# Two weight matrices loaded by a casting DMA from GpSimd instead of a plain DMA, staging tiles and cast operations

## The chip, the cores and the metric

The kernel runs on one core of one Trainium2 chip. The metric is device time in microseconds (us). TensorE is called PE, VectorE DVE, ScalarE ACT, GpSimd POOL and SyncE SP, as in the profile. A run is "fast" or "slow" by its state: a slow run took more than 1.5% longer than the fastest run of the same kernel.

## The reference, cut to what matters

```python
# attention: B=4, heads H=8, S=768, D=48; one state [D, D] for each head
for t in range(S):
    cur = einsum('bhd,bhe->bhde', u * k_t, v_t)
    y[:, :, t] = einsum('bhd,bhde->bhe', r_t, state + cur)
    state = w_t[..., None] * state + einsum('bhd,bhe->bhde', k_t, v_t)
# MLP on x = y as [3072 tokens, 384]
h = x @ w_in            # 384 x 2048
g = maximum(h, 0) ** 2
out = g @ w_out         # 2048 x 384
```

All inputs and the output are fp32 in HBM. The two weight matrices are 3.1 MB each.

## The kernel before

The 768 positions of the four sequences are cut into 24 steps of 128 tokens. A step loads four tiles (w, r, k, v) of 192 KB. Each is 1024 rows of 192 bytes, because one token of one head is 48 floats. The weights come in eight DMAs of 768 KB, with rows of 2 KB (w_in) or 1.5 KB (w_out), through the same sync queue. They land in fp32 staging tiles, and 28 copies on ACT and DVE turn them into bf16.

```python
def load_one(dst, src, b, c):                      # L69: the loads of a step
    nc.sync.dma_start(
        out=dst, in_=src[b, :, c * C:(c + 1) * C, :].rearrange("h c d -> c h d"))
...
def load_wi(g):                                    # L95; load_wo is alike
    w_st["i", g] = stage_pool.tile([C, KT, GW], FP32, name="w_st")
    nc.sync.dma_start(
        out=w_st["i", g][:],
        in_=moe_w_in[:, g * GW:(g + 1) * GW].rearrange("(a p) f -> p a f", p=128))
...
def cast(eng, kind, g, j):                         # L108
    dst = wi_sb[:, :, g * GW:(g + 1) * GW] if kind == "i" else wo_sb[:, g * 4:(g + 1) * 4, :]
    copy = nc.scalar.copy if eng == "A" else nc.vector.tensor_copy
    copy(dst[:, j], w_st[kind, g][:, j])
```

The order of instructions is not written by hand. The kernel holds a small list scheduler: each operation has an engine, an assumed duration, a rank, dependencies, and PSUM buffers that it takes or gives. While the program is built, the scheduler plays the operations through in assumed time, and each engine gets its instructions in the order found. On the chip every engine then runs its list in that order, whatever happens to the loads. Three parts matter below:

```python
# PSUM pool "cp" has ONE buffer. cum_ takes it and rd_ gives it back; p_ takes it, pm_ gives it back
op("P", .44, at, cum_, (s,), [("lw_", s)], take="cp")                  # needs w of step s
op("V", .95, at - 90, rd_, (s,), [("exp_", s), ("ld", s, "k")] + ..., give="cp")   # needs k of step s
op("P", .33, at + 5, p_, (s,), [("rkt_", s)], take="cp")
...
seq = [(0, x) for x in "wrkvu"] + [(1, x) for x in "wrkv"] + [(g, "i") for g in range(4)]
seq += [(2, x) for x in "wrkv"] + [(g, "o") for g in range(4)]
seq += [(s, x) for s in range(3, NSTEP) for x in "wrkv"]
last = []
for n, x in seq:                                   # assumed: one load after the other
    free = ...
    op("S", {"i": 2.08, "o": 2.08, "u": .65}.get(x, 1.25), 0, ld, (n, x), last + free)
    last = [("ld", n, x)]
```

The chain of one step runs: loads, cum_ (PE), exp_ (ACT), rd_ (DVE), tr_ (PE, transposes), rkt_ (DVE), p_ (PE), pm_ (DVE), y_ (PE), ysb_ (DVE), yt_ (PE), xt_ (ACT). After xt_ of a block's steps, m1_ (first MLP product) and m2_ (second) can run. The first MLP block is steps 0 and 1. In gaps before the first m2_ the scheduler inserts warm-up matmuls, whose results are not used.

## Time and profile before

The kernel before took 219.09 us (median of 2 runs, 218.32 to 219.87).

| before | value | view |
|---|---|---|
| span | 214.2 us | page |
| PE, DVE, ACT, POOL busy | 197.1, 152.7, 127.5, 84.1 us | page, busy times |
| PE busy in 0 to 40 us; of it warm-up matmuls | 35.02; 17.92 us | windows |
| first m1_ | 21.65 us | timeline of PE |
| all casts on ACT / DVE | 7.8 / 5.3 us | groups of instructions |

The first fence is the head of the page: busy time of each engine with its share of the span, then tenths of busy time (and of granted PE clock) in 40 slices.

```profile
span 214.2 us, 5655 instructions
PE 197.1 (92%) x2232; PEld 140.4 (66%) x2232; DVE 152.7 (71%) x279; ACT 127.5 (60%) x255; POOL 84.1 (39%) x105
...
PE   7898997987899997989999999999999999999983
...
PEclk9999999999999999999999999999999999999999
```

PE is the engine that sets the end: from 120 us to 205 us it is busy without a gap. So the time is decided by what PE loses earlier. The next fence is the table of windows: length, then busy time and number of instructions for each engine, granted clock, DMA share, GB/s written.

```profile
0.00:10.00 10.00, 7.78 (x50) 3.39 (x51) 3.52 (x8) 3.71 (x6) 4.59 (x15) 1.00 0.91 164
10.00:20.00 10.00, 10.00 (x97) 5.35 (x94) 7.61 (x15) 3.52 (x7) 4.89 (x7) 1.00 1.01 327
20.00:30.00 10.00, 8.98 (x89) 6.71 (x88) 7.24 (x15) 8.43 (x18) 2.89 (x3) 1.00 0.97 269
30.00:40.00 10.00, 8.27 (x99) 5.86 (x98) 6.20 (x16) 7.46 (x17) 2.28 (x3) 1.00 0.84 221
```

A busy PE is not a working PE here. Of the 35.02 us in this stretch, 17.92 are warm-up matmuls, so the useful part is 17.1 us, and 22.9 of the 40 us are lost. The DMA share shows why: the loads keep the DMA engines busy at 0.84 to 1.01. Below, idle time plus warm-up time is called *lost PE time*. Over the whole span of before it is 214.2 - 197.1 + 17.9 = 35.0 us.

The timeline of SP shows how the one queue orders the loads (start, duration, instruction; a long duration is an issue that stalls):

```profile
5.52 2.33 SPq L69 DMA_DIRECT2D rk_raw<-in_k_dram  x1
...
8.64 3.06 SPq L95 DMA_DIRECT2D w_st<-in_moe_w_in_dram  x4
11.75 0.51 SPq L69 DMA_DIRECT2D w_raw<-in_w_dram  x1
12.30 5.18 SPq L69 DMA_DIRECT2D rk_raw<-in_r_dram  x1
17.53 4.29 SPq L69 DMA_DIRECT2D rk_raw<-in_k_dram  x1
```

The loads of step 1 go ahead of the weights, and the loads of step 2 stall behind the weights for 5.2 and 4.3 us. A weight DMA takes about 1.95 us at the 400 GB/s that the windows show from 16 to 18 us (its landings lie 2.0 to 3.1 us apart, with ramps at both ends), and a step load 1.0 us, when each has the DMA engines to itself. The timeline of PE has p_ of step 1 at 16.32 and the first MLP product at 21.65:

```profile
16.32 0.40 PE L210 MATMUL cp<-rkT 64*128 64x128 bf16 x8
...
21.65 1.47 PE L288 MATMUL m<-xT,wi_sb 128*128 128x256 bf16 x12 [1.02 <-ACT xT L273]
```

### The profile page before, as it was taken

To read this page: it belongs to the slowest core of one execution; us is meant where nothing else is said; L and a number is where in the kernel's file an instruction comes from. 1 tells how busy PE (TensorE), PEld (TensorE's weight loads), DVE (VectorE), ACT (ScalarE), POOL (GpSimd) and SP (SyncE) were. 2 spreads that over 40 slices of the span, in tenths; PEclk is the share of its full clock that TensorE was granted. 3 is DMA by queue.
4 is the path that set the end of the run, shared out by engine and by line. 5 is a ranking of instruction groups with operands and counts; after the bars stand their busy time and mean duration, and the time that the engine had idled before them with its cause. 6 is when DMAs were issued, how large, how long until landed. Compare 5 with 4: busy or idle time off the path is not lost.

```text
span 214.2 us, 5655 instructions
## 1 busy us (share of the span) xinstructions
PE 197.1 (92%) x2232; PEld 140.4 (66%) x2232; DVE 152.7 (71%) x279; ACT 127.5 (60%) x255; POOL 84.1 (39%) x105
## 2 busy tenths in 40 slices
PE   7898997987899997989999999999999999999983
PEld 2454765555677675766766677777777777777751
DVE  3475795646898989879859989989886775533310
ACT  3353966644856767477685576667847546555540
POOL 5371320546556639655565655557112010000000
PEclk9999999999999999999999999999999999999999
DMA  7999899779987999699889997983101100111112
GB/s 135 195 307 344 207 383 219 153 164 193 177 152 150 181 163 171 135 200 160 172 167 195 142 203 147 193 176 76 40 2 41 37 11 28 40 37 37 40 37 73
DMA packets 107177, 30.43 MB, mean 142 GB/s; under 512 B 100368, under 2 KB 105616, under 8 KB 107152
## 3 DMA queue, kind: packets, MB, share of 16 engines
q1 hardware_dynamic: 107152, 30.09, 67.1%
q8 instruction: 17, 0.28, 0.6%
q14 instruction: 8, 0.07, 0.1%
HBM read 25.36 MB, written 4.72 MB: 140 GB/s over the span
## 4 chain that ended last, share of the span: by engine, by line
PE 46%; SPq 13%; DMA 13%; DVE 10%; issue 7%; POOL 6%; ACT 3%; DVEq 0%; POOLq 0%
PE m L307 19%; PE m L288 17%; SPq L69 10%; DMA w_st<-in_moe_w_out_dram 4%; DVE gt L300 4%; DMA w_raw<-in_w_dram 3%; DMA v_raw<-in_v_dram 3%; POOL qprod L161 2%; DVE pmT L216 2%; PE tr L198 2%; POOL ku L157 2%; DMA rk_raw<-in_r_dram 2%; POOL vq L169 2%; PE cp L210 1%; SPq L95 1%
## 5 line engine op out<-in xcount | busy, mean ns | idle before, releaser
L288 PE MATMUL m<-xT,wi_sb 128*128 128x256 bf16 (+1 forms) x672 | 76.5, 257 | 4.2 <-ACT xT L273 2.9
L295 ACT ACTIVATE rl<-m 128x512 f16<-128x512 f32 x96 | 56.5, 597 | 37.5 <-PE m L288 36.4
L307 PE MATMUL m<-wo_sb,gt 128*128 128x384 bf16 x384 | 74.9, 326 | 1.2 <-ACT o_sb L312 0.6
L288 PEld LDWEIGHTS <-wi_sb 128*128 128x128 bf16 x672 | 57.7, 98 | 17.1 <-issue 5.4
L300 DVE TENSOR_TENSOR gt<-rl 128x512 bf16<-128x512 f16 x96 | 54.7, 584 | 19.8 <-ACT rl L295 19.2
L307 PEld LDWEIGHTS <-gt 128*128 128x128 bf16 x384 | 35.3, 98 | 19.7 <-DVE gt L300 1.3
L157 POOL TENSOR_TENSOR ku<-rk_raw,u_bc 128x384 f32<-128x384 f32 x24 | 24.8, 1034 | 42.1 <-DMA rk_raw<-in_k_dram 37.3
L216 DVE TENSOR_TENSOR pmT<-cp,tri_strict 128x512 bf16<-128x512 f32 x48 | 30.8, 681 | 3.6 <-PE cp L210 3.6
L189 DVE TENSOR_TENSOR rdec_buf<-rk_raw,cp 128x768 bf16<-128x768 f32 x24 | 22.8, 948 | 11.2 <-ACT cp L185 9.0
L169 POOL TENSOR_TENSOR vq<-v_raw,q 128x384 f32<-128x384 f32 x24 | 21.6, 901 | 18.8 <-DVE y_sb L261 8.6
L161 POOL TENSOR_TENSOR qprod<-rk_raw,ku 128x384 f32<-128x384 f32 x24 | 25.1, 1048 | 1.2
L238 POOL TENSOR_TENSOR S<-t_state,a_c 128x192 bf16<-128x192 f32 x20 | 11.0, 548 | 29.3 <-DVE t_state L234 16.7
L185 ACT ACTIVATE cp<-cp 128x768 f32<-128x768 f32 x24 | 19.1, 795 | 0.8
L321 PE MATMUL m<-warm 128*128 128x512 bf16 x64 | 17.9, 416 | 1.2 <-DVE warm L129 1.2
L202 DVE COPY rkT<-tr 128x1024 bf16<-128x1024 bf16 x24 | 16.4, 682 | 3.7 <-PE tr L198 3.7
L149 ACT ACTIVATE lw_buf<-w_raw 128x384 bf16<-128x384 f32 x24 | 12.5, 521 | 8.4 <-DMA w_raw<-in_w_dram 8.2
L153 ACT CAST v_bf<-v_raw 128x384 bf16<-128x384 f32 x24 | 12.2, 508 | 8.4 <-DMA v_raw<-in_v_dram 7.7
L312 ACT ACTIVATE o_sb<-m 128x384 f32<-128x384 f32 x24 | 11.8, 491 | 8.2 <-PE m L307 7.6
L165 DVE TENSOR_REDUCE q<-qprod 128x8 f32<-128x384 f32 x24 | 13.1, 545 | 4.4 <-POOL qprod L161 4.1
L198 PE MATMUL tr<-ident,rdec_buf 128*128 128x128 bf16 x192 | 14.8, 220 | 1.3 <-DVE rdec_buf L189 1.0
L261 DVE TENSOR_TENSOR y_sb<-vq,y 128x384 bf16<-128x384 f32 x24 | 13.1, 547 | 2.2 <-PE y L255 2.1
L198 PEld LDWEIGHTS <-rdec_buf 128*128 128x128 bf16 x192 | 11.5, 98 | 4.1 <-DVE rdec_buf L189 2.0
(40 smaller groups left out, 142.9 us busy)
## 6 DMA issues: line engine op xcount, KB each, us to landing
w_raw<-in_w_dram SPq DMA_DIRECT2D x24, 192.0 KB, 4.3
rk_raw<-in_r_dram SPq DMA_DIRECT2D x24, 192.0 KB, 4.2
rk_raw<-in_k_dram SPq DMA_DIRECT2D x24, 192.0 KB, 4.3
v_raw<-in_v_dram SPq DMA_DIRECT2D x24, 192.0 KB, 4.1
out_dram<-o_sb SPq DMA_DIRECT2D x24, 192.0 KB, 2.0
w_st<-in_moe_w_in_dram SPq DMA_DIRECT2D x4, 768.0 KB, 8.5
w_st<-in_moe_w_out_dram SPq DMA_DIRECT2D x4, 768.0 KB, 8.6
u_bc<-in_u_dram SPq DMA_DIRECT2D x1, 192.0 KB, 4.6
```

Of the source, the lines that this page charges most:

```text
L69: nc.sync.dma_start(out=dst, in_=src[b, :, c * C:(c + 1) * C, :].rearrange("h c d -> c h d"))
L157: nc.gpsimd.tensor_mul(ku[:], raw["rk", s][:, 1], u_bc[:])
L161: nc.gpsimd.tensor_mul(qp[:], raw["rk", s][:, 0], tiles.pop(("ku", s))[:])
L169: nc.gpsimd.tensor_mul(vq[:], raw["v", s][:], tiles.pop(("q", s))[:, :, None].to_broadcast([C, H, D]))
L185: nc.scalar.activation(cs[:, :, 0:DM], cs[:, :, 0:DM], AF.Exp)
L189: nc.vector.tensor_mul(rdec[:, :, :, 0:D], raw["rk", s][:], tiles.pop(("cs", s))[:, :, 0:DM].rearrange("p a (h d) -> p a h d", h=H))
L198: nc.tensor.transpose(ps_tr[:, i, p, :], rdec[:, i, 2 * p:2 * p + 2, :], ident[:])
L216: nc.vector.tensor_mul(tiles["pmT", s][:, e], tiles["p", s][:, e].rearrange("p (a t) -> p a t", a=HP), tri_strict[:, None, :].to_broadcast ...
L288: nc.tensor.matmul(ps1[:, j, :], wi_sb[:, kk, n * 128:(n + 1) * 128], xT[:, kk, s0 * C:s0 * C + width], start=(kk == 0), stop=(kk == KT - 1))
L295: nc.scalar.activation(rl[:], tiles.pop(("m1", i, g))[:], AF.Relu, scale=RS)
L300: nc.vector.tensor_mul(tiles["gt", i][:, g * ng:(g + 1) * ng, :], rl[:], rl[:])
L307: nc.tensor.matmul(tiles["m2"][:], gt[:, n, mt * 128:(mt + 1) * 128], wo_sb[:, n, :], start=(n == 0), stop=(n == NT - 1))
```

## The change

The intent is to take the 28 casts off ACT and DVE, to free eight staging buffers of 6 KB per partition, and to take the weights out of the sync queue. The weights are cast during the DMA. That forces GpSimd as the issuing engine: the Trainium skill, "DMA: Bandwidth & Descriptors", section "SWDGE vs HWDGE vs iDMA", lists a cast during DMA as "SWDGE only (GpSimd)". Line numbers after the change are lower by 1 to 9.

```diff
-    stage_pool = ctx.enter_context(tc.tile_pool(name="stage", bufs=8))
...
     def load_wi(g):
-        w_st["i", g] = stage_pool.tile([C, KT, GW], FP32, name="w_st")
-        nc.sync.dma_start(
-            out=w_st["i", g][:],
+        nc.gpsimd.dma_start(
+            out=wi_sb[:, :, g * GW:(g + 1) * GW],
             in_=moe_w_in[:, g * GW:(g + 1) * GW].rearrange("(a p) f -> p a f", p=128))
...                                                   (load_wo alike; cast() and its 28 operations removed)
-            deps += [("cast", "AV"[ch % 2], "i", ch, j) for j in range(KT)]
+            deps.append(("ld", ch, "i"))
...
-    last = []
+    last, lastg = [], [("ku_", 0)]
     for n, x in seq:
         free = ...
-        op("S", {"i": 2.08, "o": 2.08, "u": .65}.get(x, 1.25), 0, ld, (n, x), last + free)
+        if x in "io":
+            op("G", 1.0, -100, ld, (n, x), lastg)
+            lastg = [("ld", n, x)]
+            continue
+        op("S", {"u": .65}.get(x, 1.25), 0, ld, (n, x), last + free)
...                                                   (in make_order)
-                           done[d] + (hop if plan[d][0] != e else 0) > now + 1e-6 for d in deps):
+                           done[d] + (hop if plan[d][0] != e else 0) > now + 1e-6
+                           for d in deps if not (e == "G" and fn is ld)):
...
-                    end = done[key] = free_at[e] = now + us
+                    end = free_at[e] = now + us
+                    if fn is ld and e == "G":
+                        landed[0] = max(landed[0], end + 1) + 4.2
+                        end = landed[0]
+                    done[key] = end
```

The last hunks are part of the change and turn out to carry about half of the loss (e3 below). The scheduler waives the dependencies of the GpSimd loads, so all eight stand ahead of the first GpSimd product. It assumes that a weight lands every 4.2 us, and that step loads beside them still take 1.25 us each.

## The prediction

> **What bounds the kernel now.** TensorE (PE). The page's busy table gives PE 92% of a 214.2 us span, DVE 71%, ACT 60%, GpSimd (POOL) 39%. By windows, it is full from 120 us to the end, so the end is set by what PE loses earlier. In 0 to 40 us PE is busy 35.0 us, but 17.9 us of that are warm-up matmuls (L321): about 23 us lost. The first MLP matmul (L288) starts at 21.65, the first of L307 at 30.8. What holds the start is loading: the DMA share is 0.84 to 1.01 in every 10 us of the first 40. A backlogged load of 192 KB moves at about 195 GB/s (1.0 us), a weight load of 768 KB at 390 to 410 GB/s (1.95 us). All DMAs go through one queue in order; the loads of step 2 wait on the sync queue for 5.2 and 4.3 us behind weights.
>
> **Removed.** 28 casts: ACT 6 x 0.61 + 8 x 0.51 = 7.8 us, DVE 6 x 0.42 + 8 x 0.35 = 5.3 us, all between 14 and 37 us, where neither engine is the limit. Worth 1 to 2 us at most: a shorter gap from landing to use.
>
> **Added.** Eight weight DMAs issued from GpSimd. In the instruction order of the changed kernel they stand, without a wait, ahead of the first ku product, so they start at about 3.5 us. I estimate 1 to 2 us of GpSimd each; the first ku, at 8.2 us today, starts at 12 to 18.
>
> **Moved.** HBM is still read for 6.3 MB of fp32 weights; only the SBUF write halves. The Trainium skill, "DMA: Bandwidth & Descriptors", "Queues, rings and completion order", says that each DMA engine alternates between queues packet by packet. A weight row is 1.5 or 2 KB, a step row 192 B, so I expect the weights to take half to four fifths of the engines until they are in, at 24 to 36 us. No trace here shows it.
>
> **The critical step.** The new order assumes step loads unaffected: it puts PE work of steps 2, 3 and 4 ahead of or between the first MLP matmuls, and PE is in order. The transposes of step 3 stand before the second MLP group. Their input cannot land before 16 loads x 1.0 + 8 x 1.95 + 1.9 = 33.5 us unless weights lag; fair shares give about 31. That makes the early MLP groups 8 to 12 us later than that order intends. Earlier weights and step loads not queued behind them win most of it back (my estimate: 7 us), so I expect a net loss of 0 to 5 us. If the two queues overlap, the loss turns into a gain of up to 7 us.
>
> **Predicted:** 220 us, 8 in 10 within 210 to 231. Faster by over 2%: 0.28; within 2%: 0.37; slower by over 2%: 0.35.
>
> **What would show it.** Right: r, k and v of steps 0 to 2 take over 6 us to land while weights are in flight; the first L288-type matmul starts after 28 us; PE idles more than 23 us in 0 to 40; the first GpSimd product after 12 us. Wrong: step loads land in 4 to 5 us beside weights and the DMA total exceeds 300 GB/s until 25 us, with MLP starting by 25 us: then about 211.
>
> **What would make it wrong.** Overlap of the two queues (faster); a cast that slows the DMA itself, or slow descriptor generation on GpSimd, delaying w_out or the first products (slower, 230); later slack that absorbs the late start.

## The result, and the profile after

The changed kernel took 226.98 us (2 runs, 226.86 and 227.10), with correct results. The ratio of fast runs is 1.047, 95% interval 1.0389 to 1.055: slower. A ratio here is the mean time of one kernel's fast runs over that of the other's of the same rounds, so it is not quite the ratio of the medians quoted.

For this pair the difference is large. The two runs of before that are listed give 226.98 / 219.09 = 1.036. The 1.047 must rest on further runs of before. The profiled one, with a span of 214.2 us, is one of these: spans lie about 2 us below times (225.1 below 227.10), so it took some 216 us (an estimate). In the four later jobs before took 215.2 to 217.1 us, which puts 226.98 at 4.5 to 5.5% over it. "Slower" holds either way; its size is good to about a point.

| | before | after |
|---|---|---|
| span | 214.2 | 225.1 us |
| useful PE time in 0 to 40 us | 35.02 - 17.92 = 17.1 | 24.45 - 18.29 = 6.2 us |
| PE idle in 40 to 150 us | 110 - 101.81 = 8.2 | 110 - 103.11 = 6.9 us |
| lost PE time, whole span | 35.0 | 225.1 - 198.3 + 18.8 = 45.6 us |
| first m1_ | 21.65 | 40.39 us |
| ACT + DVE busy | 280.2 | 264.5 us |

The casts are indeed gone: ACT and DVE together are 15.7 us less busy, of which the casts were 7.8 + 5.3 = 13.1. The span grew by 10.9 us all the same, and lost PE time grew by 10.6 us, all of it in the first 40 us. Head of the page and DMA queues of after:

```profile
span 225.1 us, 5614 instructions
PE 198.3 (88%) x2222; PEld 140.8 (63%) x2225; DVE 144.0 (64%) x265; ACT 120.5 (54%) x241; POOL 89.4 (40%) x113
...
PE   7708069999798799997999999799999999999983
...
PEclk9976658999999999999999999999999999999999
...
q1 hardware_dynamic: 103440, 23.80, 56.0%
q0 software_dynamic: 3712, 3.15, 8.7%
```

The same windows after:

```profile
0.00:10.00 10.00, 7.72 (x51) 3.48 (x53) 3.98 (x8) 3.29 (x5) 9.43 (x22) 1.00 0.92 161
10.00:20.00 10.00, 4.68 (x25) 2.04 (x25) 1.00 (x3) 1.49 (x3) 2.10 (x3) 0.72 1.23 187
20.00:30.00 10.00, 3.23 (x14) 1.33 (x12) 2.54 (x4) 0.43 (x1) 2.77 (x3) 0.67 1.18 182
30.00:40.00 10.00, 8.82 (x83) 4.63 (x86) 5.38 (x11) 3.99 (x10) 4.97 (x6) 0.75 1.02 176
```

Apart from warm-up matmuls, every compute engine is nearly empty from 10 to 30 us while the DMA share is above 1. The GB/s column counts bytes written, and a cast weight writes half of what it reads, so the fall from 327 to 187 GB/s does not mean that the reads slowed as much. The timeline of POOL shows the issues and the first products:

```profile
3.39 3.24 POOL L92 DMA_DIRECT2D wi_sb<-in_moe_w_in_dram  x4
6.62 3.00 POOL L97 DMA_DIRECT2D wo_sb<-in_moe_w_out_dram  x4
9.61 1.04 POOL L148 TENSOR_TENSOR ku<-rk_raw,u_bc 128x384 f32<-128x384 f32 x1
...
26.74 0.99 POOL L148 TENSOR_TENSOR ku<-rk_raw,u_bc 128x384 f32<-128x384 f32 x1 [14.13 <-DMA rk_raw<-in_k_dram]
```

The sync queue stalls on step loads while the weights are in flight:

```profile
5.69 5.90 SPq L68 DMA_DIRECT2D rk_raw<-in_k_dram  x1
11.63 4.07 SPq L68 DMA_DIRECT2D v_raw<-in_v_dram  x1
15.75 7.19 SPq L68 DMA_DIRECT2D w_raw<-in_w_dram  x1
22.98 4.35 SPq L68 DMA_DIRECT2D rk_raw<-in_r_dram  x1
```

**How the two queues shared the DMA engines.** Adding the time to landing to each issue, the eight weights landed at 10.6, 13.1, 15.7, 18.2, 20.8, 23.4, 26.3 and 28.9 us: 2.6 us apart, against about 1.95 alone (1.93 for casting DMAs in e1 below), so they had 75% of the engines. The step loads beside them landed at 9.4 (u), 15.8, 21.3, 26.7 (w, r, k of step 1): 6.4, 5.5 and 5.4 us apart, against 1.0 alone, or 19% from r on. The sum is 94%, so the two queues do not add up to more than one. The split is what alternation row by row gives. A DMA engine handles 24 rows of 2 KB of a w_in DMA in 1.95 us, 81 ns each, and 32 rows of a w_out DMA, 61 ns each. It handles 64 rows of a step load in 1.0 us, 16 ns each. My estimate for one for one is therefore 64 x (81 + 16) = 6.2 us for a step load beside w_in and 64 x (61 + 16) = 4.9 us beside w_out; measured is 6.4 for the load beside w_in and 5.4 beside w_out. The trace also shows the turns directly. The packets of the two queues from 10 to 26 us (queue, packets, MB, share of the engines' time) are:

```profile
q0 software_dynamic: 2911, 2.42, 93.3%
q1 hardware_dynamic: 2915, 0.55, 31.4%
```

That is one for one; but for a few packets of 4 bytes that end each DMA, a packet is a row. This agrees with the Trainium skill, "DMA: Bandwidth & Descriptors", section "Queues, rings and completion order": an engine takes turns between its queues, a packet at a time. A small row pays for a large one.

**From the late load to the late MLP.** k of step 1 lands at 26.7 instead of 11.0 us. In the table of waits of after from 8 to 40 us (engine and tile, what it waited for, total us, times, longest us), the two largest are:

```profile
DVE rdec_buf L180 <- DMA rk_raw<-in_k_dram: 16.1, 2, 15.8
POOL ku L148 <- DMA rk_raw<-in_k_dram: 14.1, 1, 14.1
```

That is a delay of 15.7 us at the start of step 1's chain, but the first MLP product is 18.7 us late. The timeline of PE after shows a second delay inside the chain:

```profile
27.80 1.03 PE L189 MATMUL tr<-ident,rdec_buf 128*128 128x128 bf16 x8 [6.03 <-DVE rdec_buf L180]
...
30.91 0.27 PE L167 MATMUL cp<-ones_col,lw_buf 128*128 128x1 bf16 x4 [1.64 <-ACT lw_buf L140]
...
35.48 0.40 PE L201 MATMUL cp<-rkT 64*128 64x128 bf16 x8
...
40.39 0.81 PE L279 MATMUL m<-xT,wi_sb 128*128 128x256 bf16 x6
```

L189 is tr_ of step 1, L167 the head of cum_ of step *2*, L201 p_ of step *1*. The timeline of DVE has the copy that p_ of step 1 needs, at 28.87, and what stands between:

```profile
28.87 0.69 DVE L193 COPY rkT<-tr 128x1024 bf16<-128x1024 bf16 x1 [0.67 <-PE tr L189]
...
33.39 0.95 DVE L180 TENSOR_TENSOR rdec_buf<-rk_raw,cp 128x768 bf16<-128x768 f32 x1 [0.35 <-DMA rk_raw<-in_k_dram]
```

p_ of step 1 had its input at 28.87 + 0.69 = 29.56, but ran at 35.48. The planned order puts cum_ of step 2 ahead of it. cum_ waits for w of step 2, which landed at 30.3. It then holds the single cp buffer until rd_ of step 2 has run, and rd_ waits for k of step 2, which landed at 33.3. rd_ ended at 34.34; the last 1.1 us before p_ are yt_ of step 0 and three warm-up matmuls, which the order also puts ahead of it. In the assumed times both loads were long in by then. This is how an order made for other landings costs time: not where the load is late, but where something that could run stands behind it.

### The profile page after: what moved, and what is told of

It reads as the page before. It is cut to its first block, busy times and chain, and to the rows that moved or that the text cites. A ratio compares the mean times of both kernels' runs of the same rounds, so it can differ in the third digit from the quotient of the medians.

```text
span 225.1 us, 5614 instructions
## 1 busy us (share of the span) xinstructions
PE 198.3 (88%) x2222; PEld 140.8 (63%) x2225; DVE 144.0 (64%) x265; ACT 120.5 (54%) x241; POOL 89.4 (40%) x113
## 3 DMA queue, kind: packets, MB, share of 16 engines
q0 software_dynamic: 3712, 3.15, 8.7%
## 4 chain that ended last, share of the span: by engine, by line
PE 58%; DMA 12%; SPq 7%; DVE 7%; issue 5%; POOL 5%; ACT 4%; DVEq 0%; POOLq 0%; ACTq 0%
PE m L279 21%; PE m L298 20%; DMA w_raw<-in_w_dram 10%; SPq L68 6%; PE tr L189 4%; PE m L312 2%; PE cp L201 2%; POOL qprod L152 2%; DVE gt L291 2%; DMA v_raw<-in_v_dram 2%; PE tr L216 2%; DVE rdec_buf L180 2%; DVE pmT L207 1%; PE tr L261 1%; PE y L238 1%
## 5 line engine op out<-in xcount | busy, mean ns | idle before, releaser
L279 PE MATMUL m<-xT,wi_sb 128*128 128x256 bf16 (+1 forms) x672 | 76.4, 257 | 0.3 <-ACT rl L286 0.3
L298 PE MATMUL m<-wo_sb,gt 128*128 128x384 bf16 x384 | 75.8, 326 | 0.7 <-ACT o_sb L303 0.6
L291 DVE TENSOR_TENSOR gt<-rl 128x512 bf16<-128x512 f16 x96 | 50.7, 538 | 27.6 <-ACT rl L286 27.5
L279 PEld LDWEIGHTS <-wi_sb 128*128 128x128 bf16 x672 | 57.9, 98 | 13.0 <-issue 0.7
L298 PEld LDWEIGHTS <-gt 128*128 128x128 bf16 x384 | 35.1, 98 | 17.8 <-issue 1.0
L160 POOL TENSOR_TENSOR vq<-v_raw,q 128x384 f32<-128x384 f32 x24 | 20.9, 870 | 26.0 <-DVE y_sb L252 14.8
L189 PE MATMUL tr<-ident,rdec_buf 128*128 128x128 bf16 x192 | 15.2, 224 | 9.0 <-DVE rdec_buf L180 8.4
L140 ACT ACTIVATE lw_buf<-w_raw 128x384 bf16<-128x384 f32 x24 | 12.6, 524 | 18.7 <-DMA w_raw<-in_w_dram 18.7
L312 PE MATMUL m<-warm 128*128 128x512 bf16 x54 | 18.8, 483 | 1.5 <-DVE warm L120 1.2
L189 PEld LDWEIGHTS <-rdec_buf 128*128 128x128 bf16 x192 | 11.6, 99 | 12.5 <-DVE rdec_buf L180 9.8
L229 POOL TENSOR_TENSOR S<-t_state,a_c 128x192 bf16<-128x192 f32 x20 | 11.3, 566 | 18.0 <-DVE t_state L225 14.7
L156 DVE TENSOR_REDUCE q<-qprod 128x8 f32<-128x384 f32 x24 | 13.1, 544 | 5.4 <-POOL qprod L152 5.3
L252 DVE TENSOR_TENSOR y_sb<-vq,y 128x384 bf16<-128x384 f32 x24 | 13.1, 545 | 1.9 <-PE y L246 1.9
## 6 DMA issues: line engine op xcount, KB each, us to landing
wo_sb<-in_moe_w_out_dram POOLq DMA_DIRECT2D x4, 384.0 KB, 17.1
```

Of the source, the lines that this page charges most:

```text
L160: nc.gpsimd.tensor_mul(vq[:], raw["v", s][:], tiles.pop(("q", s))[:, :, None].to_broadcast([C, H, D]))
L189: nc.tensor.transpose(ps_tr[:, i, p, :], rdec[:, i, 2 * p:2 * p + 2, :], ident[:])
L279: nc.tensor.matmul(ps1[:, j, :], wi_sb[:, kk, n * 128:(n + 1) * 128], xT[:, kk, s0 * C:s0 * C + width], start=(kk == 0), stop=(kk == KT - 1))
L291: nc.vector.tensor_mul(tiles["gt", i][:, g * ng:(g + 1) * ng, :], rl[:], rl[:])
L298: nc.tensor.matmul(tiles["m2"][:], gt[:, n, mt * 128:(mt + 1) * 128], wo_sb[:, n, :], start=(n == 0), stop=(n == NT - 1))
L312: nc.tensor.matmul(ps[:], warm[:, 0:C], warm[:], start=True, stop=True)
```

## The experiments

The table gives all runs first. "Lost PE" is span - PE busy + warm-up, from the profiled run; it is good to 2 or 3 us, since the ends of matmuls are modelled. The ratio compares with the kernel before of the same rounds on the same chip. All kernels gave correct results. Medians are over all runs, slow ones included. Two of the four runs of e1 and of e6 were slow; all other runs of the experiments were fast. The kernel after was not run again beside them.

| run | what | median us | ratio (95%) | lost PE us |
|---|---|---|---|---|
| before | | 219.09 | 1 | 35.0 |
| after | the change | 226.98 | 1.047 (1.039 to 1.055) | 45.6 |
| e1 | casting weights asked for late | 223.16 | 1.023 (1.018 to 1.029) | 39.0, slow run |
| e2 | early from GpSimd, no cast in flight | 232.49 | 1.075 (1.069 to 1.080) | 50.3 |
| e3 | after, planned with measured landings | 221.38 | 1.024 (1.022 to 1.026) | 41.3 |
| e4 | after, rows of 512 bytes | 230.70 | 1.068 (1.064 to 1.072) | 49.0 |
| e5 | weights behind steps 0 and 2, queue account | 214.38 | 0.989 (0.984 to 0.993) | 33.4 |
| e6 | no cast at all, sync queue | 224.21 | 1.024 (1.013 to 1.035) | 35.1 |
| e7 | as e5, weights behind steps 0 and 1 | 216.14 | 0.995 (0.989 to 1.002) | 35.1 |
| e8 | before with queue account | 215.56 | 0.995 (0.989 to 1.002) | 33.5 |
| e9 | e3 with queue account | 218.30 | 1.011 (1.005 to 1.016) | 38.1 |
| e10 | e6 with queue account | 216.61 | 1.001 (0.997 to 1.006) | 30.7 |
| e11 | e5 again, 5 rounds | 215.39 | 0.996 (0.992 to 1.000) | 34.8 |
| e12 | e5, early MLP start made possible | 216.63 | 1.006 (1.003 to 1.010) | 35.8 |

The median of before was 216.43, 217.10, 216.31 and 215.23 us in the four jobs (e1 to e4, e5 to e7, e8 to e11, e12), which ran on different chips. So ratios of different jobs carry some chip-to-chip difference.

My theory after the result was: (1) rows of weights take turns with rows of step loads, and (2) the instruction order was planned for landings that did not come. The main rival was that the casting DMA, or its issue from GpSimd, is itself slow. Where a quoted expectation uses letters, the text after it names the theory in words.

### e1: the casting DMA asked for late

The weights are issued behind the GpSimd product of step 1 (w_in) and of step 2 (w_out), at 13.2 and 20.7 us (8.6 and 22.5 in before), so that the loads of step 1 are not disturbed.

```diff
-    last, lastg = [], [("ku_", 0)]
+    last, lastg = [], {"i": [("ku_", 1)], "o": [("ku_", 2)]}
...
-            op("G", 1.0, -100, ld, (n, x), lastg)
-            lastg = [("ld", n, x)]
+            op("G", .8, -100, ld, (n, x), lastg[x] + ([("ld", n - 1, x)] if n else []))
...
-                        landed[0] = max(landed[0], end + 1) + 4.2
-                        end = landed[0]
+                        landed[0] = max(landed[0], end + 1, free_at["S"]) + 2.08
+                        end = free_at["S"] = landed[0]
```

> The casting weight DMAs stay on GpSimd, but stand behind the first ku product that needs step 1 (w_in) and step 2 (w_out); the planner books weights and step loads on one shared DMA resource. Theory A (early weights take the DMA engines from the loads of step 1): k of step 1 lands by about 13 us as before, first MLP matmul by 24 us, total 217 to 221, like before. Rival B (a casting DMA is itself slow): w_in lands over 3 us apart even where it has the engines nearly alone, first MLP matmul after 27 us, total over 223. Rival C (any DMA work on GpSimd delays its products): GpSimd products of step 1 late by 3 us or more.

Measured: 223.16 us, ratio 1.023; the profiled run was slow, the fast runs took 222.08 and 220.48. k of step 1 landed at 11.2 and the first MLP product started at 21.7, both as in before. Casting w_out DMAs, which had the DMA engines to themselves after 26.8 us, landed 1.93 us apart, against 2.1 to 2.4 for the plain w_out of before. So the cast does not slow the DMA, and rival B falls. Rival C's sign did come: the issues held GpSimd for 3.25 us, and qprod_ and vq_ of step 1 started 3.45 us later than in before (17.27 and 18.94 instead of 13.82 and 15.49). It did not delay the first MLP product. The total still missed the expectation, for a reason of my own making. The new plan set a store ahead of a step load in the sync queue (timeline of SP):

```profile
13.91 0.99 SPq L68 DMA_DIRECT2D rk_raw<-in_r_dram  x1
37.71 0.36 SPq L307 DMA_DIRECT2D out_dram<-o_sb  x1
38.12 0.43 SPq L68 DMA_DIRECT2D rk_raw<-in_k_dram  x1
```

The queue stood from 14.9 to 37.7 behind a store whose data was not ready, so k of step 3 came at 41.5. An edit to one load makes the scheduler redo the whole order, and every run below carries such side effects.

### e2: the same early issue, but no cast in flight

Weights come through GpSimd's queue as early as in after, but as fp32 into staging tiles, with the 28 casts restored.

```diff
-            out=wi_sb[:, :, g * GW:(g + 1) * GW],
+            out=w_st["i", g][:],
...                                                   (w_out alike; stage_pool, cast() and its 28 operations restored)
```

> fp32 weights go through staging tiles and the casts of before, but their DMAs are issued by GpSimd at the same early place as in the changed kernel: early second queue without a cast in flight. Theory A: loads of step 1 are as late as in the changed kernel (k of step 1 lands at 24 to 29 us), total 225 to 230. Rival B (cast in flight is to blame): step 1 lands by 15 us, total 217 to 221.

Measured: 232.49 us, ratio 1.075, worse than expected. Without a cast the step loads are starved even more: w of step 1 lands at 23.5 (15.8 in after), k at 28.2. The line of GpSimd's queue (packets, MB, share) shows a likely reason:

```profile
q0 software_dynamic: 1600, 6.29, 7.6%
```

With a cast there were 3712 packets for 3.15 MB written; without it 1600 packets for 6.29 MB, 3.9 KB each. Two or three rows then go in one packet (in the trace's list 768 packets have 4096 bytes and 640 have 4608), and a step row of 192 bytes waits for a turn of about 4 KB. The turns are again one for one: 888 packets of each queue from 10 to 20 us. The Trainium skill, "DMA: Bandwidth & Descriptors", section "SWDGE vs HWDGE vs iDMA", says that a packet holds "≤4096 B preferably, ≤64 descriptors" and is the boundary at which an engine switches; the mean of 3.9 KB agrees, and the packets of 4608 bytes show that 4096 is a preference here and not a limit. So it is not the cast that hurts. It is the early request on a second queue.

### e3: the same DMAs, planned with the landings of the trace

Only the numbers that the scheduler assumes are changed. The DMAs and their issue order are those of after.

```diff
+    took = {(0, "w"): 1.4, (0, "r"): 1.2, (0, "k"): 1.0, (0, "v"): .85, (0, "u"): 2.6, (1, "w"): 6.4,
+            (1, "r"): 5.5, (1, "k"): 5.4, (1, "v"): 2.8, (2, "w"): .8, (2, "r"): .95, (2, "k"): 2.0}
+    lands = {"i": (10.6, 13.1, 15.7, 18.2), "o": (20.8, 23.4, 26.3, 28.9)}
...
-        op("S", {"u": .65}.get(x, 1.25), 0, ld, (n, x), last + free)
+        op("S", took.get((n, x), 1.25), 0, ld, (n, x), last + free)
...
-                        landed[0] = max(landed[0], end + 1) + 4.2
-                        end = landed[0]
+                        end = lands[key[2]][key[1]]
```

> DMAs issued exactly as in the changed kernel, but the planner is given the measured landing times (w_in 10.6 to 18.2, w_out 20.8 to 28.9, step 1 at 15.8 to 29.5 us), so that no later step's work is put ahead of the first MLP groups. Theory A (late data is the cause): k of step 1 still lands at about 27, first MLP matmul at 33 to 37 instead of 40.4, total 221 to 225. Rival D (only the instruction order, planned with wrong landing times, is to blame): total 217 to 220.

Measured: 221.38 us, ratio 1.024, as expected if late data counts (221 to 225), and not the 217 to 220 of order alone. Half of the loss is gone though k of step 1 still lands at 26.3. The timeline of PE, same lines as above for after:

```profile
29.18 0.40 PE L201 MATMUL cp<-rkT 64*128 64x128 bf16 x8
...
31.71 0.25 PE L167 MATMUL cp<-ones_col,lw_buf 128*128 128x1 bf16 x4
...
33.80 1.47 PE L279 MATMUL m<-xT,wi_sb 128*128 128x256 bf16 x12
```

p_ of step 1 now stands ahead of cum_ of step 2 and runs at 29.18, not 35.48: 6.3 us earlier. The first MLP product is 6.6 us earlier and the span 5.9 us shorter. The granted clock changes too. This plan fills the wait with more warm-up matmuls (27.75 us instead of 18.8), and the clock is 1.00 throughout, where after has 0.67 to 0.75 from 10 to 40 us. What can have cost time is the work after k of step 1 came. From 24.8 to 34.9 us the clock of after is 0.50 and PE is busy for 5.23 us, which at full clock would take half: at most 2.6 us (my estimate), so part of the gain may be clock. The drop itself is stated by the Trainium skill, "TensorE: Matmul & The Clock Gate", section "Part 1: The HAM clock gate": after an idle window of about 3.4 us the clock is halved. The trace agrees: PE of after is idle from 11.2 us and the clock is 0.50 from 14.5 us on, 3.3 us later, and eleven warm-up matmuls of after at 17.2 us took 4.55 us (0.41 each), nineteen of e3 at 23.7 us took 4.26 us (0.22 each).

### e4: weights in rows of 512 bytes

If rows take turns, a shorter weight row must give the step loads more. Nine DMAs fetch the weights in rows of 512 bytes.

```diff
-        nc.gpsimd.dma_start(
-            out=wi_sb[:, :, g * GW:(g + 1) * GW],
-            in_=moe_w_in[:, g * GW:(g + 1) * GW].rearrange("(a p) f -> p a f", p=128))
+        for a, h in ([(0, 0), (0, 1)], [(1, 0), (1, 1)], [(2, 0)], [(2, 1)])[g]:
+            nc.gpsimd.dma_start(
+                out=wi_sb[:, a, :].rearrange("p (q h e) -> p h q e", h=2, e=128)[:, h],
+                in_=moe_w_in[a * 128:(a + 1) * 128, :].rearrange("p (q h e) -> p h q e", h=2, e=128)[:, h])
...                                                   (w_out: three column groups of 128)
```

> The changed kernel with the same bytes cast at the same early place, but in rows of 512 B (9 DMAs, 6 for w_in and 3 for w_out, over three times the descriptors). Theory A in its packet form (the engines take one packet of each queue in turn, so a 2 KB row against a 192 B row gives the weights three quarters): step 1 loads land about 2 to 3 us apart instead of 5.4, k of step 1 at 14 to 19 us, first MLP matmul before 33, total 218 to 223. If shares go by bytes or by time and not by packet: spacing stays near 5.4 us, k of step 1 at 25 or later, total 226 or more.

Measured: step loads landed 2.9 us apart (12.6, 15.5, 18.5, 21.4, 24.4) instead of 5.4, as taking turns foretold (6044 packets of weights against 5304 of step loads from 10 to 26 us). The total, 230.70 us (ratio 1.068), missed the expectation, and the first MLP product moved to 41.6. The weights paid with later landings (the last of w_in at 26.9, of w_out at 44.4), but w_in was in 14.7 us before that product. The old order met the cp buffer again (timelines of DVE and PE):

```profile
20.26 0.69 DVE L195 COPY rkT<-tr 128x1024 bf16<-128x1024 bf16 x1 [0.25 <-PE tr L191]
...
25.00 0.26 PE L169 MATMUL cp<-ones_col,lw_buf 128*128 128x1 bf16 x4 [4.56 <-ACT lw_buf L142]
...
32.35 0.61 PE L203 MATMUL cp<-rkT 64*128 64x128 bf16 x8 [2.97 <-DVE rdec_buf L182]
```

p_ of step 1 (L203) had its input at 20.95 and ran at 32.35, 11.4 us later: cum_ of step 2 (L169) went first, and rd_ of step 2, which frees the buffer, waited for k of step 2, landed at 31.2. So k of step 1 came 8.2 us earlier than in after, and the MLP still started 1.2 us later. The turns are confirmed; with this order they are no remedy.

### e5 and e7: weights later, and a scheduler that knows the sync queue

Two parts are changed together. The weights are issued behind early GpSimd products: in e5 w_in behind ku_ of step 0 and w_out behind that of step 2; in e7 behind qp_ of step 0 and ku_ of step 1. And the scheduler gets an account of the sync queue: an issue takes 0.6 us, a load lands later, and at most about four loads are outstanding (an estimate from the issues that stall, such as the 5.90 us above). Before, it held SP as busy until a load had landed.

```diff
+    last, lastg = [], {"i": [("ku_", 0)], "o": [("ku_", 2)]}          # e7: qp_ 0, ku_ 1
...
+                        end = landed[0] = max(landed[0], end + 2.6) + 2.5
+                    elif fn is ld:
+                        t, end = max(ring[-1], now + 1.9), 0.0
+                        got = max(0.0, landed[0] - t) * .19
+                        end = t + 5.3 if got >= 1 else max(t, landed[0]) + (1 - got) * 1.1
+                        ring.append(end)
+                        free_at[e] = max(now + .6, ring[-5] if len(ring) > 4 else 0.0)
```

> Casting DMAs on GpSimd behind the ku product of step 0 (w_in) and step 2 (w_out), with a planner that books SP issues apart from landings (about four loads outstanding, a load next to weights at a fifth of its speed), so that no store stands ahead of early loads on the sync queue, as one did in e1_late. Theory A (loss of the changed kernel = early weights plus an order planned on wrong landings, nothing else): step 1 complete by 16 us, w_in by 24, first MLP matmul at 24 to 28, PE idle between 36 and 64 us under 5 us where e1_late lost over 7, total within 1% of before. Rival C' (casting DMAs on GpSimd cost something that no order mends): at least 2% over before, as e1_late.

> As e5_ring, with w_in behind the first qprod product and w_out behind the ku product of step 1, so the weights ask for the engines 1 us later and w_out 3 us earlier. Theory A: within 1.5% of before, first MLP matmul at 24 to 29 us. Rival C': at least 2% over before.

Measured: e5 214.38 us, ratio 0.989; e7 216.14 us, ratio 0.995. The first MLP product of e5 started at 32.4, not at 24 to 28 as expected (that of e7 at 34.8, not at 24 to 29), and e5 was still the fastest kernel so far. So the start alone did not explain the gain. What differed later was the sync queue: the last step load was issued at 124.0 us, against 142.1 in before, and PE idled 3.2 us from 40 to 150 us, against 8.2. Two parts had changed at once, so controls were needed (e8, e9, e11).

### e6: no cast anywhere

To measure what the casts cost by themselves, the matmuls read the upper half of each fp32 weight as bf16 (a truncation, still within tolerance). The weights are loaded by the sync queue as in before.

```diff
+    wi_sb = wi_f[:].bitcast(BF16).rearrange("p a (f two) -> p a f two", two=2)[:, :, :, 1]
+    wo_sb = wo_f[:].bitcast(BF16).rearrange("p a (f two) -> p a f two", two=2)[:, :, :, 1]
...                                                   (loads on nc.sync into wi_f, wo_f; no casts)
```

> Kernel before without any cast and without the second queue: fp32 weights go by the sync queue straight to fp32 homes, and the matmuls read the upper halves of the words (a truncated bf16, slightly less exact). It measures what removing the 28 casts is worth by itself, with the queue as before. If casts are off the critical path: within 1% of before (the first MLP matmul earlier by under 1.5 us). If they matter: faster by 2% or more. If the matmul pays for reading every second bf16: matmuls of the two MLP lines longer than 257 and 326 ns, or weight loads longer than 98 ns, and total slower.

Measured: 224.21 us (two of four runs slow; the fast ones took 223.68 and 220.58), ratio 1.024 (unclear). The MLP started at 20.6, a little earlier than before, but the run is no clean test. The matmuls are slower with this view (m2_ 333 ns instead of 326; m1_ of 128 columns 232 instead of 219). And the new plan set the first store ahead of v of step 3 in the sync queue. Lost PE time is 35.1 us, the same as in before, so the lost time stayed although the casts were gone.

### e8 to e11: the controls

e8 is before with nothing changed but the queue account (and the assumed first times of SP and GpSimd); e9 is e3 with it, told each landing; e10 is e6 with it; e11 is e5's kernel again with 5 rounds. All four ran on the same chip beside each other. The edit of e8:

```diff
-                    end = done[key] = free_at[e] = now + us
+                    end = free_at[e] = now + us
+                    if fn is ld:
+                        end = max(ring[-1], now + 1.9) + (1.95 if key[2] in "io" else 1.1)
+                        ring.append(end)
+                        free_at[e] = max(now + .7, ring[-5] if len(ring) > 4 else 0.0)
+                        heapq.heappush(times, free_at[e])
+                    done[key] = end
```

> Control for e5_ring: kernel before (fp32 weights on the sync queue, staging tiles, 28 casts) with only the planner's account of the sync queue replaced (issue and landing apart, about four loads outstanding), so loads stand further ahead of stores. Theory E (the gain of e5_ring over before came from the order of loads and stores that the new planner made, not from the casts): as fast as e5_ring, 0.985 to 0.992 of before. Theory F (it came from the casting DMAs): 0.995 of before or slower.

> The changed kernel with its DMAs where they are, the planner told the measured landings and given the new account of the sync queue. What is left against before is the price of asking for the weights early. Theory A (half of the loss is late step data, which no order mends): k of step 1 at 25 to 28 us, first MLP matmul at 33 to 36 us, 1.01 to 1.03 of before. Rival D (order is all): 0.985 to 1.0 of before.

> As e6_upper (no cast at all, truncated fp32 read in place, sync queue) with the new account of the sync queue. In e6_upper the load of v of step 3 stood behind the first store and its PE clock fell; if that order was the cause of its loss: 0.98 to 1.0 of before. If removing the casts were worth anything on the critical path it is faster than e8_ring_before by over 0.5%; if reading every second bf16 costs: slower than e8_ring_before by 1% or more.

> The kernel of e5_ring again, five rounds, beside e8_ring_before on the same chip: 0.98 to 0.995 of before; within 0.5% of e8_ring_before if theory E holds, faster than it by 0.5% or more if F holds.

Measured: e8 215.56, e9 218.30, e10 216.61, e11 215.39 us. Four things follow.

- e8 (staged casts) and e11 (casting DMA, weights late) differ by 0.1%, where theory F asked for 0.5% or more. So the casting DMA adds nothing to e5 that these runs can see; what e5 gained over before is matched by the new order alone. By the letter of its own expectation e8, at 0.995, fell to F ("0.995 of before or slower"), but its interval (0.989 to 1.002) covers both theories, so the comparison with e11 decides. With intervals that reach 1.002 and 1.000, neither is clearly faster than before. e5's better ratio, 0.989 against 0.996 for the same kernel, is the scatter between chips and rounds.
- What the queue account changes is seen in the waits of SP from 40 to 120 us. In before, and in e3, the queue stands some 20 us behind stores that wait for their data. First before, then e3:

```profile
SPq L316 <- ACT o_sb L312: 19.5, 8, 3.7
```

```profile
SPq L307 <- ACT o_sb L303: 20.4, 9, 5.8
```

  In e8 and e9 no store waits for o_sb; all waits of stores there come to 6.0 and 3.3 us. (In after itself they were 22.3 us, 19.7 of them for o_sb.) e9, with the DMAs of after, gets from 1.024 to 1.011, its first MLP product is at 34.8, and the last step load goes out at 127.3 us.
- e9 against e8 is the price of asking for the weights early once the order fits: 218.30 against 215.56, or 1.3% (1.5% by the two ratios). Against e11, which has casting DMAs too and asks later, it is the same 1.3 to 1.5%, and the intervals (1.005 to 1.016, 0.992 to 1.000) do not overlap.
- e10 leaves open what casts cost. It is no faster than e8, but its view of the weights again makes the matmuls slower (m2_ 78.7 instead of 75.4 us in all; useful PE time 184.6 instead of 180.9). Its lost PE time is 2.8 us smaller. So without casts up to about 3 us might be won, or nothing; that is within the error of this account. It was not realised in any run.

### e12: an early MLP start and late weights

e5 started its MLP late since cum_ took the cp buffer before k had come. Here cum_ also waits for k in the plan, and the scheduler is told the landings.

```diff
-        op("P", .44, at, cum_, (s,), [("lw_", s)], take="cp")
+        op("P", .44, at, cum_, (s,), [("lw_", s), ("ld", s, "k")], take="cp")
+    seen = {("k", 1): 11.1, ("v", 1): 12.2, ("w", 2): 15.2, ("r", 2): 20.2, ("k", 2): 23.5, ...}
```

> Casting DMAs placed as in e5_ring (w_in behind the ku product of step 0, w_out behind that of step 2), planner told the landings that e5_ring showed, and not allowed to start the cumulative sum of a step (which takes the only cp bank of PSUM until k of that step is there) before that k is due. First MLP matmul at 22 to 25 us instead of 32. If the early idle of PE still sets the end: 0.97 to 0.985 of before. If the feed of later steps sets it: as e5_ring and e11_ring_again, 0.985 to 0.998.

Measured: 216.63 us, ratio 1.006 (1.003 to 1.010), outside both expected ranges. The first MLP product started at 21.1, 11 us earlier than in e5, as planned, and the kernel was no faster. w_out was issued only at 26.8 and the first m2_ came at 34.6; later steps took the time back. An early start of the MLP is not sufficient. I only argue the reason; no run separates it. No version beat before clearly: the best are e5/e11 and e8, within half a per cent to one per cent of before.

## Why the prediction was right or wrong

The measured 226.98 us lies inside the range of 210 to 231, but the centre of 220 was 7 us too low. That it lies inside owes something to a range of 21 us, which holds a gain of 4% as well as a loss of 5%. The class that came, slower by over 2%, was given 0.35, and within 2% was given 0.37.

- **"Each DMA engine alternates between queues packet by packet ... half to four fifths of the engines": right.** The weights had 75%, step loads 19%, the packets alternated one for one (2911 against 2915), and e4 halved the spacing of step loads by shortening the weight rows. The weights were in at 28.9 us, within the forecast of 24 to 36. "If the two queues overlap" did not happen: the shares add up to 94%.
- **"r, k and v of steps 0 to 2 take over 6 us to land": right for those issued beside weights** (16.3, 21.0 and 17.9 us for r, k and v of step 1; 8.2 for r of step 2), and more than I had in mind. k and v of step 2, issued as the weights ended, took 5.9 and 4.8.
- **"The new order assumes step loads unaffected": right as mechanism, and the largest single wait that the traces show.** The place differed. I had named PE work of steps 2 to 4 standing between the first MLP products. What cost 6.3 us was one place earlier: cum_ of step 2 ahead of p_ of step 1, on the single cp buffer. e3 moved it and won 5.9 us of span; in e4 the same wait was 11.4 us. That the 5.9 us are those 6.3 is argued and not shown: e3 changes the whole order and the clock, and in e12 an MLP start 11 us earlier won nothing.
- **"Win most of it back (my estimate: 7 us)": wrong. This is the step that failed.** The other term of the sum was about right: put at 8 to 12 us, it is 10.9 us of useful PE time (17.1 - 6.2) lost in the first 40 us, though counted against before and not against the order's intent. The 7 us had been worked out from no number. PE idled 6.9 us from 40 to 150 us in after, against 8.2 in before: 1.3 us won back. The loss of 0 to 5 us was 8 by the medians and 10.9 by the spans. Part of the reason is now known. The sync queue still stood behind stores for 19.5 us in before, 19.7 in after and 20.4 in e3, so step loads that no longer queued behind weights queued behind stores. Only when the scheduler accounted for that (e9) did PE idle fall to 110 - 107.69 = 2.3 us in the same stretch, from 6.3 in e3. In e8, with weights in the sync queue, the same account left 5.7.
- **"The first ku ... starts at 12 to 18": wrong, harmlessly.** It started at 9.61. I had put 1 to 2 us on GpSimd for each DMA, with no trace of such an issue to go by; it was 0.77 us.
- **"First L288-type matmul starts after 28 us": right, at 40.39.** "PE idles more than 23 us in 0 to 40" (counted with warm-up, as in the prediction): 40 - 6.2 = 33.8 us.
- **Not foreseen: the PE clock.** Idle stretches took the granted clock to 0.67 to 0.75 from 10 to 40 us; I put what it cost at 2.6 us at most.
- **"Removed ... worth 1 to 2 us at most": not refuted.** No run shows a gain from it: e11, without cast operations, equals e8, with them; e10 allows 0 to about 3 us.

Put together: of the 4.7%, planning with true landings returns 2.3 points (e3), and the order of stores and loads another 1.3 (e9). What is left against e8, which has the same account, is 1.3 to 1.5%: the price of the early request itself. It vanishes when the weights are asked for later (e11 equals e8). These are differences of ratios, and each run has a new order throughout, so the parts are good to about half a per cent, and the first to about a point, since after ran in another job than e3 and its interval is 1.039 to 1.055. How much of e3's gain is the cp buffer, the rest of the PE order or the clock is not separated by a run of its own; the waits of p_ (5.9 us in after, 4.8 of them with the buffer taken; 11.4 in e4) suggest that most is the buffer.

## What to carry to other kernels

A second DMA queue did not add bandwidth here, where the engines were full (the shares sum to 94%). It decides who waits, and when queues take turns row by row, the one with small rows loses: here a load of 192-byte rows slowed from 1.0 to 5.4 us beside weight rows of 2 KB. So ask for bulk data behind the small loads that start the first chain of work, even if its queue is free earlier. When the order of instructions is planned from assumed landing times, measure the landings after any change to the DMAs and plan again before you judge the change; and look for operations that take a single buffer and then wait for a load.

## What the Trainium skill lacked or had wrong

- "DMA: Bandwidth & Descriptors", section "Queues, rings and completion order", gives about 9 to 17 descriptors as typical for the packet that an engine drains before it switches. Here the trace counts one packet per row: the sync queue's 1024-row step loads have 64 packets on each of 16 engines, and casting weights 3712 packets, which is one for each of their 3584 rows plus 128, 16 for each DMA. From 10 to 26 us the two queues moved 2911 and 2915 packets, one for one. The page does not say what this means for two queues with rows of 192 bytes and 2 KB: shares of 19% and 75%.
- The same page, section "SWDGE vs HWDGE vs iDMA", says that a cast needs GpSimd, but neither that a cast leaves each row a packet of its own (3712 packets with it, 1600 without), nor how fast a casting DMA is: 1.93 us for 768 KB read (e1), against 2.1 to 2.4 between landings for a plain one (w_out of before).
- The same page, section "Latency and other measured facts", has a first byte after about 1 us from GpSimd and 0.6 us from sync. In the packet list of after the first packet of sync's queue starts at 1.8 us, 1.1 us after its issue began at 0.74, and the first of GpSimd's at 5.5 us, 2.1 us after its issue began at 3.39, with the sync queue loaded beside it. The first weight landed 7.2 us after its issue.
- No page gives GpSimd's own time for issuing such a DMA: 0.77 us each for 384 or 512 rows (3.00 us for four; 0.93 us for the first).
- "TensorE: Matmul & The Clock Gate", section "Part 1: The HAM clock gate", agrees with the clock seen after idle time. It puts the ramp at under 1% of a typical span. Here up to 2.6 of 225 us (an estimate) is about that 1%, but it came in the middle of the kernel after long waits for loads, and not at the start.
